# Rounded second-layer products, double-bank score tiles, moved copies, and five value loads by SyncE in a sparse attention with token routing

## The chip, the core and the metric

The program runs on one core of one Trainium2 chip. Its engines are named as the profile names them: PE (TensorE, matrix products; PEld is its loading of the stationary operand), DVE (VectorE), ACT (ScalarE), POOL (GpSimd) and SP (SyncE, which here only issues DMA transfers). A name with a q behind it (SPq, POOLq) is that engine's instruction queue. Each engine works through its own instructions in order, and engines wait for each other on semaphores. The metric is the device time of one execution in microseconds (us); smaller is better.

## What is computed

Four batches of block-sparse attention over 8 heads, 768 positions and 64 channels, and behind it a layer that routes the 128 highest-scored tokens of each batch through two dense layers. All inputs and outputs are f32.

```python
scores = scale * np.matmul(q, k.transpose(0, 1, 3, 2))
# blocks of 32; visible: |block_i - block_j| <= 1, first and last block (as row or column),
# and three sampled blocks for each block of queries (the same for all batches and heads)
scores = np.where(mask, scores, -1000000000.0)
attn = softmax(scores)                      # over the last axis
out = np.matmul(attn, v)                    # then x = out as [B, S, H * D]

scores = np.einsum('bsd,d->bs', x, w_gate)  # per token
top_idx = np.argpartition(-scores[b], 128)[:128]
xe = x[b, top_idx]
h = np.maximum(xe @ w1, 0.0)                # 512 -> 1024
ye = h @ w2                                 # 1024 -> 512
g = 1.0 / (1.0 + np.exp(-scores[b, top_idx]))
out[b, top_idx] = x[b, top_idx] + g[:, None] * ye
```

## The kernel before

**Steps.** A batch has 14 steps: three "g" steps for the first and last blocks of queries, which see all keys in three parts, and eleven units u = 1 to 11 of two query blocks each. All four batches make one list of 56 steps (`steps`, line 648). This text calls the batches one to four; the code counts b from 0. The loop from line 715 is a pipeline written out by hand: iteration s does, in this order on each engine,

- the loads and POOL work listed for s (`todo`, filled by `early`),
- `norm` of step s - 1 (DVE: divide by the sum; SP stores the rows), then the routing work listed under "a",
- `exps` of step s + 1, first half (ACT), then `turn(s)`: eight transposes of the probabilities on PE and their copies out of PSUM, the first by ACT, the second by ACT or, where `EVAC` says so (line 644), by DVE,
- `gate` of step s - 1 (DVE), routing work "c" of s - 1, `exps` of step s + 1, second half, routing work "aa", and ACT's work in `late`,
- `scores(s + 2)` and `out(s)` on PE, routing work "ab" and "b", `maxima` of step s + 2 (DVE), routing work "d".

Where nothing is late, PE is thus two steps ahead with the scores.

**PSUM.** `ps_s` holds the scores, four tiles of one bank, two to a step; `ps_t` the transposes; `ps_o` the attention output and small routing results; `ps_m` one bank for the two dense layers of batches one to three. In the last batch the dense layers use `ps_s`.

**Keys and values of a unit.** A unit's keys are gathered in SBUF into one of four buffers `kr` (line 236): two end blocks (`ends`, POOL), the four neighbouring blocks (`near`, a copy of 128 x 512, by ACT, or by POOL for u up to 4 in batches two to four), and six sampled blocks (`sampled`, POOL, at offsets that POOL loads into registers). Its values come in two parts: the fixed blocks `vs`, loaded by SP, and 2 x 128 rows `vr` (line 268), which POOL gathers from HBM with one indirect DMA for each of the unit's two query blocks (e = 0, 1) into one of seven buffers. POOL takes `gather` and `sampled` in turn, unit after unit (lines 677 to 680).

**Loads.** SP issues everything else, in program order: q two steps ahead of the scores that read it (line 685), the next batch's keys and fixed values from step 3 of the batch on (lines 686 to 690), the weights w1 and w2 (line 692), and both stores of every unit's rows. `load` ties the first transfer of a step to ACT's last instruction before it (`pace`).

**Routing.** `route(b)` places the routing of a batch into the loop by step and place (`at`, `run`): gate scores into rows and columns, ranks by comparison (`rank`, DVE), `sums`, `select`, `chosen`, `fetch` (an indirect DMA of the chosen rows by POOL). Then, from step `EXPERT[b]` on, `xt` (transpose), `h_mm` (first layer, f32), `relu` (ACT, line 582), `y_mm` (second layer, f32, line 587) and `put` (DVE, then an indirect store). The dense layers of batch one run in steps 28 to 38, of batch two in 39 to 49, of batch three in 50 to 60; those of batch four and what lies behind step 55 form the tail, in which the work is run in sorted order of step and place.

**Weights of the g steps.** `weights` (line 379) takes the running maximum over the three parts on DVE and its exponential `gw` on ACT, directly behind `next_maxima`; `join` of the next iteration begins with ACT's copy `gb`, which frees a transpose bank that PE's next transposes need.

## Time and profile before

| | us |
|---|---|
| median of three runs | 295.59 |
| the three runs | 293.88, 295.59, 297.04 |
| the profiled execution, its own time | 297.49 |
| its span, first to last instruction | 295.8 |
| mean granted PE clock | 0.991 |
| bytes read from HBM, written | 54.55 MB, 7.35 MB |

How to read the profile. The page gives for each engine the busy time, its share of the span and the number of instructions, and then the span in 40 equal slices, a digit for each slice in tenths of busy time. The chain is the work that ended last, followed back from the last instruction. In the order of time a line is start, duration, engine, line of the kernel (L66 is the helper that records every operation, so that groups are told apart by the names of their tiles), operation, output<-inputs, shape, count and, in brackets, how long the engine had been idle and what released it. In the groups the numbers behind the bar are busy time, mean nanoseconds of one and idle time before. A stretch is start:end, length, then for each engine busy time and number of instructions, the granted clock, the mean busy share of the 16 DMA engines and GB/s. An f32 product shows as two PE instructions.

### The profile page before, as it was taken

How to read it: one execution, taken by the hardware profiler on the slowest of the kernel's cores; microseconds unless marked ns; L12 is line 12 of the kernel's file. 1: busy time of each engine (PE TensorE's matmuls, PEld its weight loads, DVE VectorE, ACT ScalarE, POOL GpSimd, SP SyncE). 2: the span in 40 equal slices, each digit the busy share in tenths (PEclk: the TensorE clock that was granted, in tenths of full speed). 3: DMA queues.
4: the chain of work that ended last, by engine and by line, in shares of the span. 5: the costliest groups of instructions: out<-in, count | busy, mean ns of one | idle time of the engine just before them, and what ended most of it. 6: DMA issues, size and time to landing. Idle time of an engine off the chain costs nothing.

```text
span 295.8 us, 14282 instructions
## 1 busy us (share of the span) xinstructions
PE 259.0 (88%) x5824; PEld 192.3 (65%) x5824; DVE 204.5 (69%) x625; ACT 165.2 (56%) x392; POOL 198.2 (67%) x449
## 2 busy tenths in 40 slices
PE   3879997887988968988999999999999999889991
PEld 3456674665655745675777666787766578774890
DVE  3879886778799976884787666876995876653100
ACT  2477787563766675447467566566566576520100
POOL 5659999899998895999689616998689720011111
PEclk9799999999999999999999999999999999999998
DMA  5688899997778999989789985778466551011000
GB/s 186 232 288 265 248 361 333 331 282 213 196 211 276 288 336 367 272 275 289 239 267 296 322 254 165 241 221 219 137 177 184 141 180 39 21 39 35 38 17 19
DMA packets 33510, 62.84 MB, mean 212 GB/s; under 512 B 5284, under 2 KB 15780, under 8 KB 33444
## 3 DMA queue, kind: packets, MB, share of 16 engines
q1 hardware_dynamic: 25748, 36.39, 38.6%
q0 software_dynamic: 7696, 25.53, 28.0%
q8 instruction: 46, 0.75, 1.0%
q14 instruction: 20, 0.16, 0.2%
HBM read 54.55 MB, written 7.35 MB: 209 GB/s over the span
## 4 chain that ended last, share of the span: by engine, by line
PE 58%; DVE 20%; DMA 8%; ACT 6%; issue 5%; SPq 1%; POOLq 0%; POOL 0%; ACTq 0%; DVEq 0%
PE o L66 13%; PE h L66 10%; PE pt L66 10%; PE s L66 9%; PE y L66 8%; DVE mx L66 6%; DVE gm L66 4%; PE s_g L66 3%; DMA vr<-vt,vidx 2%; PE o_g L66 2%; DMA wbuf<-w 2%; DMA k<-kt 2%; PE pt_g L66 2%; DVE x L66 2%; ACT pr L66 1%
## 5 line engine op out<-in xcount | busy, mean ns | idle before, releaser
L66 POOL COPY kr<-k 128x128 f32 (+2 forms) x308 | 91.6, 336 | 19.1 <-DMA k<-kt 12.5
L66 POOL DMA_INDIRECT vr<-vt,vidx x88 | 89.0, 1011 | 19.4 <-issue 12.2
L66 ACT ACTIVATE pr<-s,mx 128x256 f32<-128x256 f32 x176 | 74.8, 483 | 37.0 <-DVE z L66 25.8
L66 DVE TENSOR_REDUCE mx<-s 128x2 f32<-128x512 f32 x88 | 56.5, 683 | 25.3 <-PE s L66 22.8
L66 ACT COPY pc<-pt 128x512 f32<-128x512 f32 x73 | 40.1, 592 | 17.9 <-PE pt L66 17.8
L66 PE MATMUL s<-kr,q 64*32 64x256 f32 x1408 | 48.8, 382 | 0.8 <-issue 0.8
L66 PE MATMUL pt<-ident,pr 128*128 128x128 f32 x352 | 47.2, 276 | 0.8 <-PE pt L66 0.8
L66 PEld LDWEIGHTS pt<-ident,pr 128*128 128x128 f32 x352 | 39.1, 141 | 7.2 <-issue 4.9
L66 PEld LDWEIGHTS o<-vs,pc 128*32 128x32 f32 (+1 forms) x1056 | 23.4, 118 | 27.1 <-ACT pc L66 17.8
L66 PE MATMUL o<-vs,pc 128*32 128x65 f32 (+1 forms) x1056 | 29.8, 224 | 8.8 <-ACT pc L66 3.3
L66 PE MATMUL h<-xT,wbuf 128*128 128x128 f32 x256 | 33.4, 281 | 1.3 <-ACT h L66 0.6
L66 PE MATMUL o<-vr,pc 128*32 128x65 f32 x1408 | 30.6, 222 | 3.9 <-DMA vr<-vt,vidx 2.1
L66 PEld LDWEIGHTS h<-xT,wbuf 128*128 128x128 f32 x256 | 30.1, 191 | 2.6 <-ACT h L66 0.8
L66 PE MATMUL y<-wbuf,h 128*128 128x512 f32 (+1 forms) x80 | 30.7, 521 | 0.7 <-ACT h L66 0.5
L66 PEld LDWEIGHTS s<-kr,q 64*32 64x32 f32 x1408 | 21.6, 106 | 14.2 <-issue 6.8
L66 ACT ACTIVATE pr_g<-s_g,gm 128x256 f32<-128x256 f32 x48 | 20.3, 485 | 13.8 <-DVE gm L66 9.2
L66 PEld LDWEIGHTS o<-vr,pc 128*32 128x32 f32 x1408 | 23.6, 109 | 6.1 <-DMA vr<-vt,vidx 2.4
L66 DVE CUSTOM_DVE_ANT_0 j<-x,wg_i 128x256 f32<-128x256 f32 x48 | 22.0, 459 | 0.8
L66 ACT COPY kr<-k 128x512 f32<-128x512 f32 x32 | 20.6, 643 | 0.0
L66 DVE TENSOR_TENSOR x<-o,z 128x256 f32<-128x256 f32 x44 | 18.7, 424 | 1.5
L66 PEld LDWEIGHTS y<-wbuf,h 128*128 128x128 f32 x80 | 14.1, 189 | 8.0 <-issue 5.8
L66 POOL CAST tb<-sc 128x6 bf16<-128x6 f32 x4 | 1.0, 243 | 27.3 <-DVE sc L66 27.3
(121 smaller groups left out, 309.8 us busy)
## 6 DMA issues: line engine op xcount, KB each, us to landing
vs<-vst SPq DMA_DIRECT2D x44, 260.0 KB
q<-qt SPq DMA_DIRECT2D x24, 256.0 KB
out<-x SPq DMA_DIRECT2D x88, 64.0 KB
wbuf<-w SPq DMA_DIRECT2D x16, 256.0 KB
k<-kt SPq DMA_DIRECT2D x21, 192.0 KB
vr<-vt,vidx POOLq DMA_INDIRECT x88, 4.7
k<-kt SPq DMA_DIRECT2D x3, 256.0 KB
k<-kt SPq DMA_DIRECT2D x1, 576.0 KB
```

What stands on the lines that cost most here:

```text
L66: i = getattr(self.engine, name)(*args, **kw)
```

## The change

It has these parts:

1. The score tiles become two tiles of two banks each, and one reduction takes all four maxima of a step.
2. The second dense layer is computed from rounded parts in the type float32r: w2 is split once into a rounded part (`w_high`, ACT) and the rest (`w_rest`, DVE), h in each batch likewise (`relu`: ACT the rounded part, DVE the rest), and `y_mm` multiplies high by high, high by rest and rest by high: 24 products for 8. The w2 rows are first loaded into staging tiles that share places with h; the rests lie in one key buffer and two value buffers, which the last units no longer use (`kr_at`, `vr_at`: three key buffers and five value buffers from there on). The weight loads stand at other steps.
3. `near` goes to POOL for all units of batch two and units 1 to 8 of batch three (batch four as before: 1 to 4); before, units 1 to 4 of each.
4. `EVAC` gives the second copy of every second step to DVE only in the first 14 steps (before: 28), later of every fourth.
5. The exponential of `weights` moves into `late` of the next iteration, behind both halves of `exps`.
6. `fetch` moves from place "c" to "a" of the same iteration in batches one to three, its sigmoid becomes `share` at "c", and the first subtraction of `select` becomes `ahead_of`; in the last batch the first `sums` stand one step earlier. `xt_out` and `relu` run at a new place "ar", behind `gate` and ahead of the second half of `exps`. One batch's times of `y_mm` differ.
7. In batch one the second gather (e = 1) of units 3, 5, 7, 9 and 11 becomes `plain`: SP loads three offsets into registers and issues four DMAs of 32 rows each, four steps ahead of the unit, ahead of that step's q, k and fixed value loads. DVE computes the offsets `voff` at the start.

```diff
-    ps_s = ctx.enter_context(tc.tile_pool(name="ps_s", bufs=4, space=PSUM))
+    ps_s = ctx.enter_context(tc.tile_pool(name="ps_s", bufs=2, space=PSUM))
...
+    voff = dup.bitcast(I32)[0:1]
+    vec.tensor_scalar(voff, rb[0:1], float(BLK), None, ALU.mult)
...
     def w_load(i):
         t, half = i % 4, i // 4 % 2
...
             f = i - 8
-            load(w2_s[:, f], w2[f * P:(f + 1) * P])
+            if f < 6 and f % 2 == 0:
+                t = rout.tile([P, 2, DM], F32, tag=f"h{min(f // 2, 1)}", name=f"w2_{f}")
+                stage[f], stage[f + 1] = t[:, 0], t[:, 1]
+            elif f >= 6:
+                stage[f] = rout.tile([P, DM], F32, tag="w2", name=f"w2_{f}")
+            load(stage[f], w2[f * P:(f + 1) * P])
+
+    def w_high(f):
+        act.copy(w2_h[:, f], stage[f])
+
+    def w_rest(f):
+        vec.tensor_tensor(w2_low(f), stage[f], w2_h[:, f], ALU.subtract)
...
+    KEND, VEND = 2 * NU - 4, 2 * NU - 2
+
+    def kr_at(n):
+        return n % KR if n < KEND else (n - KEND) % (KR - 1)
+
+    def vr_at(n):
+        return n % NV if n < VEND else (n - VEND + 1) % (NV - 2)
...
+    def w2_low(f):
+        tag, i = (("w2_0", 0) if f < 1 else (f"kr{KR - 1}", f - 1) if f < 4 else (f"vr{NV - 2 + (f - 4) // 2}", f % 2))
...
     def ahead(b, u):
-        return b and u <= 4
+        return u <= (0, NU - 1, 8, 4)[b]
...
+    def plain(u):
+
+        with tc.issue_after(sp.last):
+            _, o = nc.values_load_multi_w_load_instructions(
+                voff[0:1, 2 * u, :], engines=[SP], min_val=0, max_val=NB * BLK,
+                skip_runtime_bounds_check_because="sampled blocks index the blocks of the sequence")
+        j = NB if u == NU - 1 else 2 * u + 1
+        for i, rows in enumerate([slice(j * BLK, (j + 1) * BLK)] + [ds(x, BLK) for x in o]):
+            sp.dma_start(vr_of(0, u)[BLK * i:BLK * (i + 1), 1], vt[rows, :])
...
-        st[t] = [ps_s.tile([P, 2, 8, BLK], F32, tag="s", name=f"s{b}_{t[1]}_{t[-1]}_{g}") for g in range(G)]
+        st[t] = ps_s.tile([P, G, 2, 8, BLK], F32, tag="s", name=f"s{b}_{t[1]}_{t[-1]}")
...
-        for g in range(G):
-            vec.tensor_reduce(mx[:, g], st[t][g].rearrange("p h k c -> p h (k c)"), AX.X, ALU.max, negate=True)
+        vec.tensor_reduce(mx.rearrange("p g h -> p (g h)"), st[t].rearrange("p g h k c -> p (g h) (k c)"), AX.X, ALU.max,
+                          negate=True)
...
-        act.activation(d, d, AF.Exp)
+        late.setdefault(steps.index((b, "g", c)) - 1, []).insert(0, lambda: act.activation(d, d, AF.Exp))
...
-    Y_AT = ((7, 7, 8, 8, 9, 9, 10, 10),) * 2 + ((7, 8, 9, 9, 10, 10, 10, 10), (5, 5, 6, 6, 7, 7, 8, 8))
+    Y_AT = ((7, 7, 8, 8, 9, 9, 10, 10),) * 2 + ((7, 9, 9, 10, 10, 10, 10, 10), (5, 5, 6, 6, 7, 7, 8, 8))
...
+        def ahead_of():
+            R["rs"] = rout.tile([P, T], F32, tag="rs", name=f"rs{b}", bufs=2)
+            vec.tensor_tensor(R["rs"], later, R["cp"], ALU.subtract)
...
         def relu(k):
-            if k == 0:
-                R["h"] = rout.tile([P, 8, P], F32, tag="h", name=f"h{b}")
-            act.activation(R["h"][:, 4 * k:4 * k + 4], R["pm"], AF.Relu)
+            h = R["h", k] = rout.tile([P, 2, 4, P], F32R, tag=f"h{k}", name=f"h{b}_{k}")
+            act.activation(h[:, 0], R["pm"], AF.Relu)
+            vec.scalar_tensor_tensor(h[:, 1], R["pm"], 0.0, h[:, 0], ALU.max, ALU.subtract)
...
-            pe.matmul(R["y"][:, 0:c.stop - c.start], R["h"][:, f], w2_s[:, f, c], start=f == 0, stop=f == 7)
+            parts = [(0, f, w2_h[:, f, c]), (0, f, w2_low(f)[:, c])]
+
+            parts += [(1, i, w2_h[:, i, c]) for i in ((f,) if f < 4 else () if f < 7 else range(4, 8))]
+            for n, (i, j, w) in enumerate(parts):
+                pe.matmul(R["y"][:, 0:c.stop - c.start], R["h", j // 4][:, i, j % 4], w,
+                          start=f == 0 and n == 0, stop=f == 7 and n == len(parts) - 1)
...
-        plan += [(c, "c", lambda: rank(5)), (c if last else c + 1, "ab", lambda: sums(0, T - 1)),
-                 (c + 1, "ab", lambda: sums(T - 1, T)), (c + 1, "c", select), (c + 2, "ab", chosen), (c + 2, "c", fetch)]
+        plan += [(c, "c", lambda: rank(5)), (c - 1 if last else c + 1, "ab", lambda: sums(0, T - 1)),
+                 (c + 1, "ab", lambda: sums(T - 1, T)), (c + 1, "c", select), (c + 2, "ab", chosen)]
+        plan += [(c + 1, "bb", ahead_of), (c + 2, "c", fetch)] if last else [(c + 2, "a", ahead_of), (c + 3, "a", fetch), (c + 2, "c", share)]
...
-        return steps.index(t) % (2 if steps.index(t) < EXPERT[0] else 4) == 0
+        return steps.index(t) % (2 if steps.index(t) < per else 4) == 0
...
+    PLAIN = (3, 5, 7, 9, 11)
...
         for e in range(2):
-            early(at_, lambda b=b, u=u, e=e: gather(b, u, e))
+            if b == 0 and e and u in PLAIN:
+                early(max(at_, first[n] - 4), lambda u=u: plain(u))
+            else:
+                early(at_, lambda b=b, u=u, e=e: gather(b, u, e))
...
-    for i in range(16):
-        early((22 if i < 4 else 21 if i < 8 else 22) + i, lambda i=i: w_load(i))
+    for i, at_ in enumerate((20, 21, 22, 23, 27, 28, 29, 30, 24, 25, 26, 28, 33, 33, 31, 34)):
+        early(at_, lambda i=i: w_load(i))
+    for f, at_ in enumerate((31, 31, 32, 32, 34, 34, 33, 36)):
+        late.setdefault(at_, []).append(lambda f=f: w_high(f))
+        at(at_, "d", lambda f=f: w_rest(f))
...
+        run(s, "ar")
         run(s - 1, "c")
```

More of the change, by code (lines that the diff above doesn't have):

```diff
@@ L8 @@
 F32 = mybir.dt.float32
+F32R = mybir.dt.float32r
 BF16 = mybir.dt.bfloat16
@@ L16 @@
 POOL = mybir.EngineType.Pool
+SP = mybir.EngineType.SP
 ACT = mybir.EngineType.Activation
@@ L216, in load_gate @@
             sp.dma_start(wg_i[64 * g:64 * g + 64], wg2[:, g * 256:(g + 1) * 256].broadcast_to([64, 256]))
-    wbuf = const.tile([P, 2 * DM * FF // P], F32, name="wbuf")
-    w1_s = wbuf[:, 0:DM * FF // P].rearrange("p (t f) -> p t f", f=FF)
-    w2_s = wbuf[:, DM * FF // P:].rearrange("p (f c) -> p f c", c=DM)
+    w1_s = const.tile([P, DM // P, FF], F32, name="w1_s")
+    w2_h = const.tile([P, FF // P, DM], F32R, name="w2_h")
+    stage = {}
     def w_load(i):
@@ L228, in w_load, with user_of, vr_of @@
             f = i - 8
-            load(w2_s[:, f], w2[f * P:(f + 1) * P])
-    offs = {}
-    kbuf = [const.tile([P, 14, KW], F32, name=f"kr{i}") for i in range(KR)]
-    def kr_of(b, u):
-        return kbuf[(b * (NU - 1) + u - 1) % KR]
+            if f < 6 and f % 2 == 0:
[8 more added lines that the diff above has]
+        vec.tensor_tensor(w2_low(f), stage[f], w2_h[:, f], ALU.subtract)
+    offs = {}
+    kbuf = [const.tile([P, 14, KW], F32, tag=f"kr{i}", name=f"kr{i}") for i in range(KR)]
+    KEND, VEND = 2 * NU - 4, 2 * NU - 2
[3 more added lines that the diff above has]
+        return n % NV if n < VEND else (n - VEND + 1) % (NV - 2)
+    def user_of(place, n):
+        return max((i for i in range(n) if place(i) == place(n)), default=None)
+    def kr_of(b, u):
+        return kbuf[kr_at(b * (NU - 1) + u - 1)]
+    vbuf = [const.tile([P, 2, VR], F32, tag=f"vr{i}", name=f"vr{i}") for i in range(NV)]
+    def vr_of(b, u):
+        return vbuf[vr_at(b * (NU - 1) + u - 1)]
+    lows = {}
+    def w2_low(f):
+        tag, i = (("w2_0", 0) if f < 1 else (f"kr{KR - 1}", f - 1) if f < 4 else (f"vr{NV - 2 + (f - 4) // 2}", f % 2))
+        if tag not in lows:
+            n = DM if f < 1 else 14 * KW if f < 4 else 2 * VR
+            lows[tag] = const.tile([P, n], F32R, tag=tag, name=f"low_{tag}")
+        return lows[tag][:, DM * i:DM * (i + 1)]
     def offsets(b, u):
@@ L253, in ahead @@
     def ahead(b, u):
-        return b and u <= 4
+        return u <= (0, NU - 1, 8, 4)[b]
     def ends(b, u):
-        if u <= KR:
+        if u <= (KR if b < 2 else KR - 1):
             for at in (4, 8):
@@ L302, in scores @@
                         qe = q[rows, p].rearrange("d e c -> d (e c)") if ne == 1 else q[rows, p, e]
-                        pe.matmul(st[t][g][r0:r0 + w, ph], qe, keys(rows, e, slice(p * BLK, (p + 1) * BLK)),
+                        pe.matmul(st[t][r0:r0 + w, g, ph], qe, keys(rows, e, slice(p * BLK, (p + 1) * BLK)),
                                   start=ph == 0, stop=ph == 1, tile_position=(64 * g, r0), skip_group_check=True)
@@ L362, in out @@
             return
-        parts = [(1 if b < 2 else 2, lambda e: vs_of(b, t[1])), (2, lambda e: vrs[b, t[1]][:, e])]
+        parts = [(1 if b < 2 else 2, lambda e: vs_of(b, t[1])), (2, lambda e: vr_of(*t)[:, e])]
         for c, (ne, v) in enumerate(parts):
@@ L552, in fetch, with share @@
                     vec.tensor_scalar(R["put"][:, half:half + 1], ts[:, 0:1], 2.0, float(half), ALU.mult, ALU.add)
+            R["ts"] = ts
+            if last:
+                share()
+        def share():
             ge = R["ge"] = rout.tile([P, 1], F32, tag="ge", name=f"ge{b}", bufs=2)
-            act.activation(ge, ts[:, 1:2], AF.Exp, scale=-1.0)
+            act.activation(ge, R["ts"][:, 1:2], AF.Exp, scale=-1.0)
             vec.tensor_scalar_add(ge, ge, 1.0)
@@ L558, in mid @@
         def mid(name):
-            pool = (ps_s, "s") if b == B - 1 else (ps_m, "m")
-            return pool[0].tile([P, 512], F32, tag=pool[1], name=f"{name}{b}").rearrange("p (t c) -> p t c", t=4)
+            if last:
+                m = ps_s.tile([P, 1024], F32, tag="s", name=f"{name}{b}")[:, 0:512]
+            else:
+                m = ps_m.tile([P, 512], F32, tag="m", name=f"{name}{b}")
+            return m.rearrange("p (t c) -> p t c", t=4)
         def xt():
@@ L671, in block_sparse_attention_moe @@
         m = n + 2 if b == 0 else n
-        at_ = max(first[m - KR] - 1 if m >= KR else 0, first[n - NV] + 1 if n >= NV else 0, b2 * per - 3)
+        k_, v_ = user_of(kr_at, m), user_of(vr_at, n)
+        at_ = max(0 if k_ is None else first[k_] - 1, 0 if v_ is None else first[v_] + 1, b2 * per - 3)
         if b:
@@ L677, in block_sparse_attention_moe @@
         for e in range(2):
-            early(at_, lambda b=b, u=u, e=e: gather(b, u, e))
+            if b == 0 and e and u in PLAIN:
+                early(max(at_, first[n] - 4), lambda u=u: plain(u))
+            else:
+                early(at_, lambda b=b, u=u, e=e: gather(b, u, e))
             if u2 < NU:
```

14 lines of the change are left out of this document (5 added, 9 removed).

## The prediction

> **What bounds the kernel now.** I read the page first (shares, slices, chain), then the stretches of the four batches, then the order of time where TensorE idles, then the groups by shape for prices. Work runs in 56 steps, 14 to a batch (3 global, 11 units); a stretch below starts at the first transpose of its batch.
>
> ```profile
> span 295.8 us, 14282 instructions
> PE   3879997887988968988999999999999999889991
> POOL 5659999899998895999689616998689720011111
> PE 58%; DVE 20%; DMA 8%; ACT 6%; issue 5%; SPq 1%; POOLq 0%; POOL 0%; ACTq 0%; DVEq 0%
> ```
>
> ```profile
> core 0: us, PE busy (x) PEld busy (x) DVE busy (x) ACT busy (x) POOL busy (x), PEclk, DMA share, GB/s
> 12.10:67.50 55.40, 48.42 (x1238) 34.86 (x1239) 43.89 (x131) 40.29 (x96) 47.03 (x102) 1.00 0.89 290
> 67.50:126.90 59.40, 49.76 (x1275) 35.76 (x1273) 50.12 (x149) 37.36 (x91) 51.75 (x117) 1.00 0.87 272
> 126.90:196.90 70.00, 66.14 (x1567) 49.62 (x1566) 50.44 (x158) 42.59 (x101) 52.48 (x116) 1.00 0.81 254
> 196.90:258.40 61.50, 59.30 (x1449) 44.89 (x1448) 44.90 (x141) 38.87 (x92) 34.71 (x75) 1.00 0.50 146
> 258.40:295.80 37.40, 29.11 (x247) 22.52 (x245) 8.78 (x30) 3.98 (x9) 5.36 (x8) 0.98 0.09 29
> ```
>
> Batches three and four are TensorE's: busy 66.14 of 70.00 us and 59.30 of 61.50. There only fewer matmul microseconds help. In batch one TensorE idles 7.0 us (55.40 - 48.42), in batch two 9.6 us; in two VectorE (50.12) and POOL (51.75) are as busy as TensorE, so those waits come from them. The last stretch is a serial tail: route the last tokens, fetch, two matmul layers, store.
>
> **The change part by part.**
>
> *Five gathers leave POOL (units 3, 5, 7, 9, 11 of batch one).* Around the sixth to eighth unit POOL never rests, and TensorE waits for a gather that POOL issued late:
>
> ```profile
> 42.64 0.98 POOL L66 DMA_INDIRECT vr<-vt,vidx  x1 [0.16 <-issue]
> 43.61 0.76 POOL L66 COPY kr<-k 128x128 f32 x3
> 44.54 0.98 POOL L66 DMA_INDIRECT vr<-vt,vidx  x1 [0.16 <-issue]
> ```
>
> ```profile
> 44.54 6.73 DMA vr<-vt,vidx
> ```
>
> ```profile
> PE o L66 <- DMA vr<-vt,vidx: 2.1, 2, 1.7
> PE pt_g L66 <- ACT gb L66: 3.0, 3, 1.2
> ```
>
> A gather takes POOL 0.98 + 0.16 = 1.14 us, so five free 5.7 us of the 47.03. Only two waits, 2.1 us in all, are ended by a gather; at most the whole 7.0 us idle could go, at least nothing. I take 2.1: two of the removed gathers precede the first wait, three the second, so POOL is 2.3 to 3.4 us earlier there, more than the waits.
>
> What they become is put on SyncE: per unit a register load and four copies of 32 rows, 25 instructions, placed ahead of that step's q, k and value loads and its output stores.
>
> ```profile
> 39.92 0.53 SPq L66 DMA_DIRECT2D k<-kt  x1
> 40.49 0.48 SPq L66 DMA_DIRECT2D vs<-vst  x1
> 41.07 1.12 SPq L66 DMA_DIRECT2D out<-x  x2
> 43.15 0.33 SPq L66 DMA_DIRECT2D q<-qt  x1
> 9.37 0.18 DVE L66 TENSOR_SCALAR koff<-rb 1x72 int32<-1x72 f32 x1
> L243 POOLq TENSOR_LOAD <-koff x44: 1384/1395/2465, 9.6 to 233.0; - x44
> ```
>
> No SyncE register load is in the trace; the nearest row is POOL's, 1.4 us. It costs nothing if it runs behind other issues, 2.5 us at worst. Four issues at 0.45 us (between the 0.33 of q and the 0.56 of an output store) are 1.8 us; together 3.2 us every second step. SyncE issues 0.53 + 0.48 + 1.12 = 2.1 us a step, 2.3 with its half share of a q load; two steps at TensorE's 3.3 us hold 6.6, and the demand becomes 4.6 + 3.2 = 7.8. So SyncE falls 1.2 us behind in every pair of steps, 4 to 5 us by the tenth step. Behind it wait q (issued two steps, 6.6 us, ahead of its scores, of which a landing as slow as the 6.73 above leaves nothing, one of 4 some 2 us) and batch two's k and fixed value loads. I charge +1.0 us, from 0 (backlog hidden) to +3. The offsets themselves cost VectorE one more multiply like koff's, 0.18 us at the start; between 0 and that, I book 0.
>
> The Trainium skill, DMA: Bandwidth & Descriptors, section "Issuing engines are not separate DMA queues", speaks against this part: the same 16 engines move the bytes whoever issues, so only issue time is saved. By that rule alone the 2.1 us would be 0, and the sum 2.1 us less; the trace is open on it, for issue time is what POOL lacked, while the bytes are the same.
>
> *Weights' exponentials later (gw).* ScalarE now waits for VectorE's weight before it copies gb, and TensorE's next transposes wait for that copy: 3.0 us in three waits (row above). With gw behind the next exps, gb starts when its matmuls are done. I take 2.0 of the 3.0, 0.7 in each of batches one to three (rounded in the sum); 0 if another wait ends last.
>
> *One maximum reduction over two banks, fewer VectorE evacuations, near copies to POOL, two score tiles of double size instead of four.*
>
> ```profile
> L66 DVE TENSOR_REDUCE mx<-s 128x2 f32<-128x512 f32 x88 | 56.5, 683 | 25.3 <-PE s L66 22.8 <-ACT pr L66 2.1
> L66 DVE COPY pc<-pt 128x512 f32<-128x512 f32 x15 | 10.3, 685 | 5.6 <-PE pt L66 5.5
> L66 POOL COPY kr<-k 128x512 f32<-128x512 f32 x12 | 7.4, 617 | 0.0
> L66 ACT COPY kr<-k 128x512 f32<-128x512 f32 x32 | 20.6, 643 | 0.0
> 98.65 1.01 POOL L66 COPY kr<-k 128x128 f32 x3
> 102.34 0.88 PE L66 MATMUL s<-kr,q 64*32 64x256 f32 x24
> ```
>
> A pair of reductions occupies 56.5/44 = 1.28 us; one of 1024 columns is 683 + 512 more columns (0.53 at the pair's slope, 0.6 busy each), 1.21, so 0.07 saved a step: 1.0 in batch two. Batch two loses four evacuations (steps 14, 18, 22, 26 go to ScalarE): 4 x 0.685 = 2.7. Of this 3.7 us of VectorE's 50.12 I let half shorten the batch, 1.9. ScalarE takes four copies and gives up seven near copies of 643 ns. Both tiles of a step were already waited for together, so the tiles cost nothing.
> POOL gets those seven near copies: 7 x 0.617 = 4.3 us, in a batch where it is 87% busy. For the eighth unit its copies end at 99.66, TensorE reads them at 102.34: margin 2.7 us. POOL enters batch two some 3 us earlier (5.7 freed, less a wait for the k loads that SyncE's backlog makes late), and by unit eight has spent 4 x 0.617 = 2.5 of it. So the margin is 3.2 us, and that caps what both batches gain together: of -2.1 + 1.0 - 0.7 - 1.9 - 0.7 = -4.4 I book **-3.2**. In batches three and four POOL has room (its ring shrinks to three key and five value buffers; at 52.48 of 70.00 and 34.71 of 61.50 busy I cost that at nothing; uncovered, each late unit would cost its 1 us gather).
>
> *The second layer in rounded parts.* Eight f32 products of 512 columns become 24 (high x high, high x low, low x high).
>
> ```profile
> L66 PE MATMUL y<-wbuf,h 128*128 128x512 f32 x48 | 23.7, 616 | 0.7 <-ACT h L66 0.5 <-issue 0.2
> L66 PE MATMUL y<-wbuf,h 128*128 128x256 f32 x32 | 7.1, 379 | 0.0
> 166.60 1.82 PE y L66 x4
> 172.04 1.91 PE y L66 x4
> L66 DVE SCALAR_TENSOR_TENSOR xe<-y,ge,xe 128x512 f32<-128x512 f32 x3 | 2.3, 751 | 2.7 <-PE y L66 2.7
> L66 DVE TENSOR_TENSOR ga<-ga,gb 128x260 f32<-128x260 f32 x8 | 3.6, 456 | 0.8
> 144.40:163.20 18.80, 18.42 (x480) 14.77 (x479) 15.08 (x49) 12.04 (x27) 16.05 (x36) 1.00 0.85 268
> ```
>
> An f32 product is two instructions (48 for 24 products) of 0.455 to 0.478 us: 16 x 0.466 = 7.46 us a batch. The new type is in no row. Bounds: 0.455 an instruction (as now) or half, 0.228 (if one instruction that no longer splits the moving operand streams at twice the pace). I take 0.228: the pair shows an f32 operand being split, and the other operand should be split alike. Then 24 x 0.228 = 5.47, -2.0 a batch, **-4.0** for the experts of batches one and two, which run in the TensorE-bound stretches. It breaks even at 7.46/24 = 0.311 us.
> The Trainium skill, FP8 and Floating Point Precision, section "TensorE Precision Notes", counts four passes for true FP32; a quarter of the 0.93 us product is 0.23, the lower bound again; no run here shows it.
> Added: eight ScalarE roundings of w2 (643 ns each, 5.1 us, steps 31 to 36) and eight VectorE subtractions: 456 ns at 260 columns plus 252 more columns is 0.72, 5.8 us. Also two VectorE low parts per batch at 0.75. In 144.4 to 163.2 (steps 31 to 34) VectorE is free 3.7 us of 18.8; seven subtractions and a low part bring 5.8: it overruns by about 2. I charge **+2.0** (0 if steps overlap, 4 if the order chains them). ScalarE (12.04) has 6.8 us free and gives up four near copies in this batch. SyncE's loads for f = 4, 5, 7 wait for the subtractions of the step before; out stores queue behind; x has six buffers: nothing.
> Relu and xT copies moved ahead of the second exps end TensorE waits of about 0.5 us; gw gives 0.6: batches three and four together -4.0 + 2.0 - 0.6 - 0.5 = **-3.1**.
>
> *The tail.*
>
> ```profile
> 266.22 0.52 PE L66 MATMUL scp<-one_b,M 128*128 128x1 bf16 x15
> 266.60 1.10 PE L66 MATMUL y<-wbuf,h 128*128 128x512 f32 x2
> 267.54 0.29 PE L66 MATMUL scp<-one_b,M 128*128 128x1 bf16 x6
> 267.87 0.16 DVE L66 TENSOR_TENSOR rs<-later,scp 128x6 f32<-128x6 f32 x1 [1.86 <-PE scp L66]
> 274.88 7.42 PE L66 MATMUL h<-xT,wbuf 128*128 128x128 f32 x64 [0.46 <-ACT xT L66]
> ```
>
> The first sums move one place up and batch three's y products leave the gap before the last sums: rs, 1.86 us late, comes 1.0 earlier, and the fetch with it. The first layer (7.42) stays. The last y, 7.1 us for 32 instructions, becomes 48 of 256 columns; half of 0.222 is 0.111, but 64 loads and products of 128 columns take 7.42/64 = 0.116, which I take as the floor: 5.57, -1.5. The low parts finish under the products. Tail **-2.5**.
>
> Sum: -3.2 - 3.1 - 2.5 = **-8.8 us**. The profiled execution took 297.49 us (span 295.78 and 1.7 around it), so 288.7; it stands 1.9 above the median of the three runs, 295.59. Against the median: **286.8 us**.
>
> **The rivals.**
> 1. *Neither POOL nor VectorE limits.* SyncE hides the loads, POOL stays ahead, the w2 work overlaps: -2.8 in batch one, -4.4 in two, -5.1 in three and four, -2.5: -14.8, **280.8 us**. For it: the copies' margin is still 2.7 us where POOL is deepest in batch two. Against: margin has to carry 4.3 us of new copies.
> 2. *The moved rows are late all the same*, on SyncE's queue or on the DMA engines (0.89 busy in batch one, the bytes unchanged). Then batches one and two give nothing: -5.6, **290.0 us**; with q late too, 292. For it: 7.8 us of issue in 6.6.
> 3. *The other side: the new products stream no faster than an f32 instruction.* One mechanism: 24 x 0.455 = 10.9 a batch, +3.5 instead of -2.0, for two batches +11 against my sum; in the tail 48 x 0.217 = 10.4, +3.3 instead of -1.5, and the gap before the sums fills again, +1.5. Total +8.5: **304.1 us**. It decides above 0.311 us an instruction. For it: no f32 row here passes a column in under 0.89 ns (0.455 us for 512). Against: only that the operands are rounded to one part, which the trace does not show.
>
> **How the numbers follow.** Forecast 0.47, rival one 0.18, rival two 0.20, rival three 0.08, something else 0.07. Range 280 to 294 us: it takes in rivals one and two and leaves out rival three and half of the rest. About 1% (3 us) is what a measurement of this kernel can tell from no change: faster is below 292.6. That is nearly all of the forecast, all of rival one and most of two: 0.77; within 1%, the ends of two and some of the rest, 0.12; slower, rival three and the rest, 0.11.
>
> **What would show each step.** y instructions near 0.23 us and 72 plus 48 of them; no TensorE wait for vr at the seventh unit; SyncE's issues in steps 3 to 9 and whether scores wait for q; POOL's last key copies of batch two against the scores; VectorE overrunning in steps 31 to 36; rs one microsecond sooner after the last rank. Wrong would be: y at 0.45, scores waiting for q or kr for more than 3 us, or batch one not shorter.

## The result and the profile after

| | before | after |
|---|---|---|
| median, us | 294.00 (293.62 to 297.04, 6 runs) | 299.69 (297.42 to 301.52, 6 runs) |
| ratio, 95% interval | | 1.0147 (1.0104 to 1.019) |
| the profiled execution, us | 297.49 | 299.08 |
| its mean granted clock | 0.991 | 0.97 |

The change made the kernel slower by 1.5%. The prediction, 286.8 us with a range to 294, was wrong in size and in sign. The medians lie 5.7 us apart, the two profiled executions only 1.6: the one of before was 3.5 us above its median, the one after 0.6 below. The traces below therefore show where 1.6 us went; the other 4.1 are in no trace. On two chips of the experiments the same kernel was faster than before; that comes further down.

The page of the changed kernel: shares, two engines and the clock in slices, and its chain, which breaks off at the last store and so says nothing here.

```profile
span 297.4 us, 14386 instructions
PE   3899897949888899998997989999999999998891
POOL 6649998229999999999789685991888783003111
PEclk9999997987999999999997999999999999999996
issue 1%; POOLq 0%; DMA 0%
```

The stretches of the four batches and the tail, cut at the first transposes of each as before.

```profile
core 0: us, PE busy (x) PEld busy (x) DVE busy (x) ACT busy (x) POOL busy (x), PEclk, DMA share, GB/s
12.03:73.94 61.91, 53.19 (x1239) 38.35 (x1239) 43.55 (x117) 39.91 (x96) 42.55 (x100) 0.92 0.84 260
73.94:130.54 56.60, 50.53 (x1275) 36.30 (x1273) 48.90 (x132) 35.82 (x88) 52.72 (x113) 1.00 0.88 282
130.54:201.28 70.74, 66.73 (x1575) 53.24 (x1574) 56.17 (x153) 44.52 (x104) 58.71 (x125) 0.98 0.81 257
201.28:261.90 60.62, 58.26 (x1456) 46.63 (x1455) 44.06 (x127) 38.58 (x93) 34.49 (x75) 1.00 0.50 143
261.90:297.40 35.50, 26.94 (x271) 23.77 (x269) 11.61 (x37) 3.97 (x9) 5.34 (x8) 0.94 0.10 30
```

Batch one is 6.5 us longer (61.91 against 55.40), batch two 2.8 shorter, batch three 0.7 longer, batch four 0.9 shorter, the tail 1.9 shorter. Together +1.6, the difference of the two profiled executions. POOL's busy time in batch one fell from 47.03 to 42.55 as intended, and two of its slices show a 2: it waits there. The clock of batch one is 0.92 where it was 1.00.

In the order of time, TensorE's two long waits of batch one, then SyncE's queue around them, then POOL:

```profile
46.72 1.63 PE L68 MATMUL s<-kr,q 64*32 64x256 f32 x32 [2.65 <-DMA q<-qt]
66.19 1.99 PE L68 MATMUL s_g<-k,q 64*64 64x256 f32 x16 [4.13 <-DMA q<-qt]
```

```profile
38.95 3.30 SPq L68 DMA_DIRECT2D vr<-vt  x4
42.37 1.18 SPq L68 DMA_DIRECT2D q<-qt  x1
...
48.28 3.37 SPq L68 DMA_DIRECT2D vr<-vt  x4
51.75 0.37 SPq L68 DMA_DIRECT2D q<-qt  x1
...
58.12 3.95 SPq L68 DMA_DIRECT2D vr<-vt  x4
62.17 0.37 SPq L68 DMA_DIRECT2D k<-kt  x1
62.59 0.42 SPq L68 DMA_DIRECT2D vs<-vst  x1
63.06 0.42 SPq L68 DMA_DIRECT2D q<-qt  x1
```

```profile
64.78 1.29 POOL L68 COPY kr<-k 128x256 f32<-128x256 f32 x3 [10.89 <-DMA k<-kt]
```

Scores wait for q, 2.65 us in step 8 (7.40 us long, 4.02 before) and 4.13 us in step 12 (9.24 us, 3.26 before). The q loads that should go out as steps 6, 8 and 10 begin (35.86, 42.98 and 53.80 us here) go out at 42.37, 51.75 and 63.06: 6.5, 8.8 and 9.3 us behind. In the kernel before, the q load of step 8 goes out at 43.15, 0.5 us after the step begins. A row `vr<-vt x4` holds a unit's register load and its four issues. From one such row to the next, 38.95 to 48.28, SyncE works without a pause for 9.3 us, while the two steps 6 and 7 take 7.1. The next batch's last keys go out at 62.17, and POOL, which had gained its head start, loses it in one wait of 10.89 us.

Each wait is paid twice: within 2 us of its end the granted clock halves, for one or two stretches of 3.41 us. Three stretches, cut where the clock changes:

```profile
47.16:50.57 3.41, 3.41 (x75) 2.31 (x58) 1.47 (x3) 0.40 (x2) 3.08 (x11) 0.50 1.02 371
64.22:71.05 6.83, 4.86 (x68) 3.45 (x69) 2.55 (x5) 0.76 (x2) 5.70 (x14) 0.50 0.89 253
159.80:163.21 3.41, 3.41 (x16) 3.41 (x17) 3.27 (x9) 0.84 (x2) 3.24 (x7) 0.50 1.04 373
```

That is 13.65 us at half clock. In batch one TensorE is busy for 8.3 us of it, work that takes about half of that at full clock: some 4 us, an estimate from these rows. The third stretch is step 33 (8.72 us, 5.14 before). There VectorE and ScalarE show why:

```profile
152.77 0.68 DVE L68 SCALAR_TENSOR_TENSOR h<-h,h 128x512 fp32r<-128x512 f32 x1
153.37 0.70 DVE L68 SCALAR_TENSOR_TENSOR M<-sb,sc,before 128x384 bf16<-128x384 f32 x1
...
154.00 0.74 DVE L68 SCALAR_TENSOR_TENSOR M<-sb,sc,before 128x512 bf16<-128x512 f32 x1
...
154.67 1.21 DVE L68 TENSOR_REDUCE mx<-s 128x4 f32<-128x1024 f32 x1
...
156.12 1.28 DVE L68 TENSOR_TENSOR low_kr<-w,w_h 128x512 fp32r<-128x512 f32 x2
```

```profile
156.30 0.84 ACT L68 ACTIVATE pr<-s,mx 128x256 f32<-128x256 f32 x2 [2.38 <-DVE mx L68]
```

The low part of h and two comparisons stand ahead of the reduction whose maxima ScalarE waits for, 2.38 us, and two rests of w2 follow it; products of step 33 stand behind ScalarE.

The groups that answer to the prices of the prediction (busy, mean ns of one, idle before):

```profile
L68 DVE TENSOR_REDUCE mx<-s 128x4 f32<-128x1024 f32 x44 | 53.6, 1219 | 23.7 <-PE s L68 22.4 <-issue 1.2
L68 DVE SCALAR_TENSOR_TENSOR h<-h,h 128x512 fp32r<-128x512 f32 x8 | 5.5, 690 | 14.0 <-ACT h L68 12.8 <-ACT pc L68 1.2
```

The merged reduction takes 1.22 us (1.21 forecast). The low parts of h take 0.69 each, and VectorE waits 12.8 us for ScalarE ahead of them. Of the waits for ScalarE's gb, 3.0 us before, TensorE has none of its own left.

### The profile page after: what moved, and what is told of

Same layout as the page of the kernel before. It is cut to its first block, busy times and chain, and to the rows that moved or that the text cites. A ratio compares the mean times of both kernels' runs of the same rounds, so it can differ in the third digit from the quotient of the medians.

```text
span 297.4 us, 14386 instructions
## 1 busy us (share of the span) xinstructions
PE 262.3 (88%) x5864; PEld 203.0 (68%) x5864; DVE 210.4 (71%) x582; ACT 164.9 (55%) x393; POOL 200.6 (67%) x451
## 2 busy tenths in 40 slices
DMA packets 34069, 62.83 MB, mean 211 GB/s; under 512 B 5524, under 2 KB 16020, under 8 KB 34004
## 5 line engine op out<-in xcount | busy, mean ns | idle before, releaser
L68 POOL COPY kr<-k 128x128 f32 (+2 forms) x315 | 97.9, 348 | 29.4 <-DMA k<-kt 12.6
L68 POOL DMA_INDIRECT vr<-vt,vidx x83 | 83.5, 1006 | 21.0 <-issue 12.0
L68 DVE TENSOR_REDUCE mx<-s 128x4 f32<-128x1024 f32 x44 | 53.6, 1219 | 23.7 <-PE s L68 22.4
L68 PE MATMUL s<-kr,q 64*32 64x256 f32 x1408 | 50.6, 385 | 4.0 <-DMA q<-qt 2.8
L68 PE MATMUL h<-xT,w_s 128*128 128x128 f32 x256 | 34.7, 289 | 0.9 <-ACT xT L68 0.5
L68 PEld LDWEIGHTS h<-xT,w_s 128*128 128x128 f32 x256 | 31.6, 200 | 2.1 <-ACT xT L68 0.7
L68 PE MATMUL y<-w_h,h 128*128 128x512 f32 (+1 forms) x80 | 23.5, 364 | 0.8 <-DVE sc L68 0.8
L68 PE MATMUL s_g<-k,q 64*64 64x256 f32 x192 | 16.4, 472 | 7.9 <-DMA q<-qt 4.1
L68 DVE TENSOR_REDUCE gm<-s_g 128x4 f32<-128x1024 f32 x12 | 14.7, 1222 | 11.5 <-PE s_g L68 11.5
L68 PEld LDWEIGHTS o_g<-vs,pc_g 64*64 64x64 f32 x384 | 13.8, 136 | 7.8 <-ACT pc_g L68 5.1
```

The source lines that it names most:

```text
L68: i = getattr(self.engine, name)(*args, **kw)
```

## The experiments

Eighteen measurements were made on five chips, called A to E; some kernels ran on several. On A, B, C and E the kernel before took 314 to 319 us, on D 295. So ratios are always to the kernel before on the same chip, and absolute times are compared within one chip only.

| kernel | chip | before, us | this, us | ratio, 95% interval |
|---|---|---|---|---|
| without the five loads | A | 318.46 | 312.48 | 0.9851 (0.9749 to 0.9952) |
| before, with the five loads alone | A | 318.46 | 317.97 | 0.9986 (0.9942 to 1.0031) |
| loads behind q, k and values | A | 318.46 | 308.31 | 0.970 (0.9589 to 0.981) |
| loads of fixed rows | A | 318.46 | 308.65 | 0.9717 (0.9635 to 0.9799) |
| the whole change | B | 318.87 | 309.51 | 0.9808 (0.9691 to 0.9925) |
| without the five loads | B | 318.87 | 310.83 | 0.9824 (0.9695 to 0.9953) |
| before, with the five loads alone | B | 318.87 | 318.02 | 0.9989 (0.9925 to 1.0052) |
| loads behind q, k and values | B | 318.87 | 309.25 | 0.9732 (0.9602 to 0.9861) |
| the whole change | C | 314.00 | 309.29 | 0.985 (0.9802 to 0.9898) |
| loads behind, ranks sooner | C | 314.00 | 310.16 | no interval given |
| the same, relu on VectorE | C | 314.00 | 309.09 | 0.9849 (0.9768 to 0.993) |
| the kernel before, once more | C | 314.00 | 315.36 | one run |
| nine loads instead of five | D | 295.06 | 310.97 | 1.0537 (1.0481 to 1.0593) |
| less work in batch one, five loads | D | 295.06 | 296.36 | 1.0032 (0.9988 to 1.0076) |
| less work in batch one, no loads | D | 295.06 | 291.23 | 0.9867 (0.9802 to 0.9932) |
| the second layer in f32 | D | 295.06 | 299.36 | 1.0151 (1.0079 to 1.0222) |
| without the five loads | E | 314.40 | 309.83 | 0.9861 (0.9806 to 0.9916) |
| the same, ranks sooner, relu on VectorE | E | 314.40 | 307.03 | 0.9768 (0.9716 to 0.9821) |

**Without the loads, and the loads alone (chip A).** The first takes the seventh part out of the change:

```diff
-    PLAIN = (3, 5, 7, 9, 11)
+    PLAIN = ()
```

> The whole change but for its seventh part: all second gathers of batch one stay on POOL. Theory A (the loads that SyncE now issues delay q and the next keys, and the granted clock falls behind the waits): batch one is back near 55 us, no half clock before step 33, no score product waits for q; 291 to 294 us, against 299.7 for the whole change and 294 before. Rival B (the other six parts make it slow): 297 or more, with the same waits of PE in another place of batch one.

The second puts `plain`, `voff` and the branch in the list of gathers into the kernel before, and nothing else.

> The kernel before with the seventh part alone. Theory A: PE waits for q in steps 8 to 12, two windows of half clock, batch one 4 to 7 us longer than its 55.4; 298 to 301 us. Rival B: within 1 us of before, 293 to 295.

Neither answer of theory A came: on this chip the loads alone cost nothing (317.97 against 318.46), and the change without them is 1.5% faster than before. Rival B does not hold either: it asked for a version without the loads slower than before. And before takes 318 us here, 24 more than in the result, so this is another condition.

**Order and amount of SyncE's work (chip A).** The loads are registered behind those of their step, or read fixed rows without the register load:

```diff
-                early(max(at_, first[n] - 4), lambda u=u: plain(u))
+                behind.append((max(at_, first[n] - 4), u))
...
+    for s, u in behind:
+        early(s, lambda u=u: plain(u))
```

> The whole change, with each unit's register load and four issues placed behind that step's q, k and value loads in SyncE's order instead of ahead of them. If the order in the queue is what hurts, q is issued some 3 us sooner in the steps that have both, and half or more of the loss comes back: 294 to 296 us, with the keys of batch two still late. If it is the total time of issue, or the bytes on the DMA engines, that hurts: 298 to 300.

```diff
-        with tc.issue_after(sp.last):
-            _, o = nc.values_load_multi_w_load_instructions(
...
-        for i, rows in enumerate([slice(j * BLK, (j + 1) * BLK)] + [ds(x, BLK) for x in o]):
+        for i, rows in enumerate([slice(j * BLK, (j + 1) * BLK)] + [slice(x * BLK, (x + 1) * BLK) for x in (2 * u - 1, 2 * u, 2 * u - 3)]):
```

> The whole change, with the four loads of 32 rows at fixed addresses and no register load; it reads other rows, so the values of these blocks are not the sampled ones, but the bytes are the same. SyncE saves the load of 0.7 to 0.9 us and the register arithmetic, about 1.2 of some 3.3 us for each of the five. If the issue time counts, the demand of 7.8 us in 6.6 falls to 6.6: 294 to 296 us. If the bytes on the DMA engines count, or the wait for the buffer: 298 to 300.

308.3 and 308.7 us, but the whole change had no time on this chip, so these two decide nothing by themselves.

**The whole beside its parts (chip B).** No new edit.

> The whole change, unaltered, beside its parts on one chip. The chip of the first four kernels ran the kernel before in 318.5 us, with 11 to 14 us of TensorE waits that nothing in the profile ends, so only kernels of one chip are compared. Theory A (the loads ahead of the queue cost 5 to 7 us, the rest gains): slower than before by 1 to 2%, and slower than the same change without these loads by 1.5 to 3%. Rival B (the other six parts make it slow): the same time as without these loads, within 1%.

> The whole change without its seventh part, again, beside the whole change. Theory A: 1.5 to 3% under the whole change, 0.5 to 1.5% under the kernel before. Rival B: level with the whole change. Rival D (the loads help once they are behind the queue, as 308.3 against 312.5 us on the first chip hints): above the version with the loads behind by 1%.

> The kernel before with the seventh part alone, again. On the first chip it was level with the kernel before (ratio 0.9986, 0.9942 to 1.0031), which speaks against theory A, if waits of another kind did not hide the loss there. Theory A: 1 to 2.5% slower than before here. Rival B: level again.

> The whole change with the loads behind the q, k and value loads of their step, again, beside the whole change. If the order in SyncE's queue is the cause: 1 to 2% under the whole change and under the kernel before. If the amount of issue or the bytes are: level with the whole change.

The whole change is 1.9% faster than before here, level with the version without the loads (309.5 and 310.8) and with the loads behind (309.3). Theory A, as first stated, has fallen: the same loads cost nothing on this chip. What differs is above all TensorE's pace. Rows of SyncE's queue in the whole change on chip B:

```profile
42.04 0.36 SPq L68 DMA_DIRECT2D q<-qt  x1
47.87 3.28 SPq L68 DMA_DIRECT2D vr<-vt  x4
51.43 0.19 SPq L68 DMA_DIRECT2D q<-qt  x1
56.47 3.55 SPq L68 DMA_DIRECT2D vr<-vt  x4
61.24 0.42 SPq L68 DMA_DIRECT2D q<-qt  x1
```

These q loads go out at 42.0, 51.4 and 61.2 us, hardly sooner than in the result (42.4, 51.8, 63.1). But steps 6, 8 and 10 begin at 38.36, 46.10 and 55.94 instead of 35.86, 42.98 and 53.80, so the loads are 3.7, 5.3 and 5.3 us behind and the scores hardly reach them: the only wait for q in batch one is 1.1 us. In the kernel before with the loads alone the q loads of these steps are 4 to 7 us late on chips A and B, and scores wait 1.5 and 2.6 us for them.

**Why chips A, B, C and E are slower.** The kernel before was profiled on chip C, beside the whole change and two repairs.

> The whole change once more, beside the kernel before and two changed versions on one chip. On the second chip it was 2% faster than before (309.5 against 318.9 us), on the chip of the result 1.5% slower. Theory A' (the loads ahead of the queue cost time only where TensorE is fed without gaps: there the steps last 3.3 us and SyncE's demand of 7.8 us does not fit into two of them; where gaps stretch the steps to 3.8 us and more, it fits): if before runs near 294 us here, this one is slower than it by 1 to 2% with stalls for q in steps 8 and 12; if before runs near 318, it is 1 to 3% faster and those stalls are under 2 us. Rival C (the stalls come from chance, not from the pace): slow in some executions of both chips alike, so its own times here spread by 5 us or more.

> The kernel before, for its trace on this chip. If it runs near 294 us, TensorE's waits that nothing ends are 5 us as in the profile shown; if near 318, some 12 us, spread over batches one to three, and the steps of batch one last 3.8 us or more in the mean.

Step 49 of the kernel before, on TensorE: first in the profile shown ahead of the prediction, then on chip C.

```profile
233.51 0.67 PE L66 MATMUL o<-vs,pc 128*32 128x65 f32 x32
234.00 0.64 PE L66 MATMUL o<-vr,pc 128*32 128x65 f32 x32
```

```profile
249.12 0.73 PE L66 MATMUL o<-vs,pc 128*32 128x65 f32 x16
250.27 0.33 PE L66 MATMUL o<-vs,pc 128*32 128x65 f32 x4 [0.42 <-issue]
251.00 0.44 PE L66 MATMUL o<-vs,pc 128*32 128x65 f32 x12 [0.40 <-issue]
251.23 0.67 PE L66 MATMUL o<-vr,pc 128*32 128x65 f32 x32
```

The same 64 products take 1.1 us in the one and 2.8 us in the other, with gaps in which TensorE waits for nothing that is recorded. In the list of waits of before on chip C and in the profile shown, in this order, this kind of wait is:

```profile
PE o L66 <- issue: 9.8, 24, 1.1
```

```profile
PE o L66 <- issue: 1.8, 1, 1.8
```

Over all tiles such waits are 5.4 us in the profile shown, 2.1 in the result, 1.3 to 4.6 on chip D, and 11 to 15 on A, B, C and E. What makes them is open: the packets of the largest DMA queue take 0.071 us in the mean on A and B as in both profiles of the result, which speaks against slower transfers, and no experiment was made on it. Batch one of the kernel before lasts 64.3 us on chip C and 55.4 in the profile shown. Of these 8.9 us such gaps make up 3.7 (4.2 against 0.5), and the granted clock is 0.95 instead of 1.00; the rest is not explained.

The other two kernels of chip C test step 33, both with the loads behind as well:

```diff
-            plan += [(c, "c", lambda: rank(0)), (c + 1, "c", lambda: rank(1)), (c + 2, "c", lambda: rank(2)),
+            one = int(b == 1)
+            plan += [(c, "c", lambda: rank(0)), (c + 1 - one, "c", lambda: rank(1)), (c + 2 - one, "c", lambda: rank(2)),
...
```

> The whole change with the loads behind q, k and values in their step, and with the comparisons `rank(1)` and `rank(2)` of batch two one step sooner, so that VectorE has one comparison of 0.70 us less in the step ahead of step 33. If VectorE's queue is what makes step 33 long (8.7 us in the result, 7.0 on the second chip, 5.1 before), it falls by 0.7 us or, where half clock goes too, by 3: 0.3 to 1% under the whole change, and 2% or more under it on a chip on which the loads hurt. If something else makes it long, it stays at 7 or more.

```diff
-            act.activation(h[:, 0], R["pm"], AF.Relu)
+            if b:
+                vec.tensor_scalar(h[:, 0], R["pm"], 0.0, None, ALU.max)
+            else:
+                act.activation(h[:, 0], R["pm"], AF.Relu)
```

> As the kernel with the sooner ranks, and in batches two to four VectorE computes the rounded part of h too, so that its low part does not wait for ScalarE (12.8 us of such waits, the longest ahead of the last stretch 2.5 us). If that wait delays the maxima, steps 43, 44, 46 and 47 are shorter by 1 us together or more; if VectorE's added 0.68 us each takes that back, the time is level.

Step 33 goes from 7.05 us to 6.66 and 6.62, so VectorE's queue sets part of it, but by less than the 0.7 us expected, and the times stay level (310.2 and 309.1 against 309.3). With the relu on VectorE steps 43, 44, 46 and 47 change by -0.1, -0.6, +0.1 and +0.3 us, 0.3 shorter together, not the 1 us expected if the wait for ScalarE delayed the maxima there. The whole change itself is 1.5% faster than before on this chip, with one wait for q of 2.3 us. Its times spread by 7.6 us, which rival C would ask for, but those of before spread by 6.8, so the spread tells nothing.

**The dose and the pace (chip D).** This chip runs the kernel before in 295.06 us, as in the result. The first kernel uses the loads for all of the units 3 to 11; the next two leave products out of batch one so that it runs faster:

```diff
-    PLAIN = (3, 5, 7, 9, 11)
+    PLAIN = tuple(range(3, NU))
```

> The whole change with the loads by SyncE for all nine units 3 to 11 of batch one instead of every second. SyncE's demand is then 2.3 + 3.2 = 5.5 us a step. Theory A' (SyncE's issue time against TensorE's pace): it fits into no pace, the backlog grows by 1.5 us in each of nine steps even at 4 us a step, and TensorE waits for q or the next keys for 8 us or more in all: 6 to 14 us above the whole change. Rival C (the stalls were chance): within 2 us of the whole change, with POOL 4 us freer.

```diff
-        for c, (ne, v) in enumerate(parts):
+        for c, (ne, v) in list(enumerate(parts))[int(b == 0):]:
...
```

> The whole change, with the value products of the fixed rows left out in the units of batch one (half of each unit's value products), so that TensorE has less to do there and reaches the pace of 3.3 us a step or less that it had in the result. Theory A': stalls for q appear near steps 8 and 12 as in the result, of 4 us or more in sum, and batch one is no shorter than the 58.7 us of the whole change on the third chip, or by less than 3. Rival C: no such stalls, batch one some 5 us shorter.

The third is the same with `PLAIN = ()`.

> The same products left out, without the loads by SyncE. Theory A': no wait for q; batch one shorter than that of the kernel with the loads by 3 us or more, if POOL's second gathers (some 50 us of work) do not become the bound; if they do, TensorE waits for gathered rows or key copies instead, and the two are level within 2 us. Rival C: level with no stall in either.

Nine loads take 310.97 us, 15.9 above before, where five took 5.7. The dose acts, and it acts where theory A' says: stretches of batch one with nine loads, and the waits for q and key copies in it.

```profile
12.02:82.97 70.95, 54.12 (x1239) 38.23 (x1239) 43.01 (x117) 40.22 (x96) 38.40 (x97) 0.86 0.77 228
```

```profile
PE s_g L68 <- DMA q<-qt: 5.1, 1, 5.1
PE s L68 <- DMA q<-qt: 5.0, 1, 5.0
PE s L68 <- POOL kr L68: 3.4, 1, 3.4
```

POOL is freer than ever (38.40 us) and the DMA engines idler (0.77 of their time, 228 GB/s), yet the stretch is the longest of all. So neither POOL nor bytes bound it; SyncE's queue does, in which the q loads of steps 6, 8 and 10 go out 11 to 15 us late.

The pair with less work shows the price of the five loads on one chip: 296.36 with them, 291.23 without, 5.1 us between the medians. The two profiled executions differ by only 0.8 us (291.86, the fastest of its ten, and 291.11), so their stretches show where time moves, not the whole price. Batch one and batch two with the loads, then without:

```profile
12.13:69.72 57.59, 46.34 (x1062) 31.77 (x1063) 43.61 (x117) 39.56 (x96) 42.30 (x99) 0.94 0.87 272
69.72:125.67 55.95, 50.49 (x1278) 36.02 (x1274) 48.34 (x132) 35.58 (x88) 52.04 (x113) 1.00 0.90 295
```

```profile
13.01:65.34 52.33, 43.21 (x1062) 29.75 (x1062) 42.75 (x117) 39.76 (x96) 44.22 (x95) 0.97 0.90 298
65.34:124.23 58.89, 50.91 (x1276) 36.18 (x1274) 49.50 (x132) 35.58 (x88) 54.65 (x119) 1.00 0.88 282
```

Batch one is 5.3 us longer with the loads, batch two 2.9 us shorter. Two points of what was expected were not met. The 58.7 us named there is not batch one of the whole change on chip C, which took 62.8, so the comparison with that chip says little; the one with the next kernel does. And only 0.9 us of TensorE's wait is put down to q with the loads. Waits for transposed tiles are alike in both (4.7 and 4.2 us), and a wait of 1.9 us for a key copy of ScalarE is there only with the loads; so this pair shows a price, but not by itself that q is what carries it. The q loads are again 5.3 to 8.9 us behind their steps with the loads (40.56, 49.16 and 59.35 for steps that begin at 35.27, 42.16 and 50.49) and at most 1.4 without. Without them waits for gathered rows appear, 2.6 us, as theory A' had allowed.

**The second layer (chip D).** The whole change with w2 and h left as f32 and eight products:

```diff
-            parts = [(0, f, w2_h[:, f, c]), (0, f, w2_low(f)[:, c])]
-
-            parts += [(1, i, w2_h[:, i, c]) for i in ((f,) if f < 4 else () if f < 7 else range(4, 8))]
+            parts = [(0, f, w2_h[:, f, c])]
...
```

> The whole change with the second layer in f32 as before (eight products, no rounding of w2 or h on ScalarE and VectorE). By the prediction's terms: 2.0 us more in each of batches two and three's stretches and 1.5 in the tail, 2.0 less in steps 31 to 36: 3.5 us above the whole change. By what the result showed (0.64 us gained in steps 46 to 49, step 33 longer by 3.6): steps 31 to 36 2 us or more shorter, steps 46 to 49 under 1 us longer, the tail 1.5 to 2 longer: level with the whole change within 1.5 us.

Its ratio, 1.0151, is level with that of the whole change in the result, 1.0147, within 0.8%: no gain of the rounded layer is seen at this pace. Batch one, which has no product of that layer, is here a second trace of the five loads beside their queue: it lasts 59.7 us, the q loads of steps 6, 8 and 10 go out 6.7, 8.4 and 8.9 us late, and TensorE waits for them three times:

```profile
PE s L68 <- DMA q<-qt: 5.5, 3, 2.4
```

The tail is 0.7 us longer than in the result (36.21), not 1.5. By stretches, steps 31 to 36 and steps 39 to 49 of this kernel:

```profile
147.04:174.88 27.84, 27.82 (x702) 20.92 (x701) 22.97 (x66) 16.44 (x38) 24.25 (x53) 1.00 0.84 270
184.71:237.56 52.85, 51.80 (x1223) 38.70 (x1221) 39.53 (x112) 32.26 (x78) 40.56 (x88) 1.00 0.60 176
```

Steps 31 to 36 with the rounded layer (the kernel with nine loads, same chip, clock 1.00), and steps 39 to 49 of the result:

```profile
159.06:189.32 30.26, 27.52 (x706) 21.77 (x705) 28.39 (x76) 20.36 (x46) 26.93 (x55) 1.00 0.81 257
```

```profile
187.26:240.10 52.84, 51.53 (x1230) 40.66 (x1229) 39.78 (x114) 32.00 (x77) 40.23 (x86) 1.00 0.60 175
```

In steps 31 to 36 VectorE goes from 22.97 of 27.84 us to 28.39 of 30.26: it becomes the busiest engine, and the steps are 2.4 us longer. In steps 39 to 49 the two are equal to 0.01 us, although the products are cheaper: TensorE's time in them falls by 1.3 us in steps 46 to 49 (7.73 to 6.44), and its busy time over all eleven steps by only 0.3.

**The two repairs together (chip E).** Without the loads, and the same with the sooner ranks and the relu on VectorE.

> The whole change without the loads by SyncE. If before runs near 295 us here: theory A' gives batch one 55 to 57 us instead of 61.9, no wait for q, 293 to 295 us, ratio 0.99 to 1.00, where the whole change has 1.0147; rival B gives 1.01 or more. If before runs near 315: 0.98 to 0.985 as on the first two chips, which adds nothing.

> As m1, with two comparisons of batch two one step sooner and the rounded part of h on VectorE in batches two to four. If VectorE's queue took the gain back: step 33 shorter by 0.7 us or, where half clock goes too, by 3; steps 46 and 47 shorter by 0.5 us together; 1 to 4 us under m1, the fastest of all where before runs near 295. If it is something else: level with m1 within 1 us.

Before takes 314.4 us here, so the first adds nothing on the pace, as said. 307.03 against 309.83 us; the intervals (0.9716 to 0.9821 and 0.9806 to 0.9916) just overlap. Steps 33, 44, 46 and 47 are shorter by 0.35, 1.4, 1.0 and 0.5 us, step 48 is longer by 0.6: less than expected in step 33, more in 46 and 47. On chip C the same relu made steps 46 and 47 0.4 us longer together, so this gain is not shown to be its doing. The tail is 1.4 us longer (37.38 against 35.97). From the start of the last batch's first layer (283.41 and 290.06 us) both need 20.0 us to the end, so the difference lies ahead of it, where this kernel has 3.41 us at half clock (from 275.15) and the other none. Of the versions without the loads it is the fastest by ratio; with the loads behind their queue, A and B gave 0.970 and 0.973. None of these was run where before takes 295 us, so none is shown to beat both kernels there.

## Why the prediction was wrong

**The five loads.** The step that failed is "So SyncE falls 1.2 us behind in every pair of steps, 4 to 5 us by the tenth step [...] I charge +1.0 us, from 0 (backlog hidden) to +3". The mechanism was named, q and the next keys behind a full queue, and even the margin was there, some 2 us. The size was wrong. The price of a unit's loads was right (3.3 to 4.0 us for a register load and four issues, 3.2 forecast), but the rest of SyncE's work in two steps came to 6.0 us instead of 4.6, so SyncE falls 2.2 us behind in a pair of steps (9.3 of work in 7.1, steps 6 and 7), not 1.2, and the queue is 5.0 us behind already at the fourth step, 6.5 at the sixth and 9.3 at the tenth. The two waits for q are 6.8 us where +1.0 was charged. The prediction's terms for batch one add up to -1.8 us (-2.1, +1.0, -0.7); measured is +6.5, a miss of 8.3 and the largest of all. Batch two was to give -2.6 and gave -2.8. For the whole kernel the pair on chip D puts the five loads at 5.1 us by its medians. Rival two saw the right place and stopped at "batches one and two give nothing".

The Trainium skill, DMA: Bandwidth & Descriptors, section "Issuing engines are not separate DMA queues", says that another issuing engine saves issue time alone, and that this time is usually small beside the transfer. The trace agrees with the first and not with the second: the bytes are the same (62.84 and 62.83 MB), and the register load and four issues, 3.3 to 4.0 us a unit, fill a queue on which batch one waits.

**The clock.** No term stood for it. Two waits for q of 2.65 and 4.13 us put 10.2 us of batch one at half clock, some 4 us by the estimate above.

**The second layer's products.** Their rate was right: 0.23 us for 512 columns, and the last y fell from 7.1 us to 6.0 (5.6 forecast). The step that failed is "-4.0 for the experts of batches one and two, which run in the TensorE-bound stretches". Steps 35 to 38 and 46 to 49 gained 0.3 to 0.9 us instead of 2.0 each. Part of it is size: TensorE's time in these products fell by 1.3 us a batch, not 2.0. In steps 31 to 36 VectorE becomes the busiest engine with the low parts and the rests of w2. What holds back steps 46 to 49 is open: the low parts wait for ScalarE there, but taking that wait away made steps 46 and 47 together 1.5 us shorter on chip E and 0.4 longer on chip C. The charge for the rests, +2.0, was right (2.4 on chip D), and half clock in step 33 came on top in the result.

Rival three rested on a reading that does not hold: the last y of the kernel before passes 256 columns in 0.22 us, 0.86 ns each, so a row under 0.89 ns was there.

**Right in number.** Batch two is 2.8 us shorter, and POOL's copies were in time (TensorE waits 0.7 us for them). That the merged maxima, fewer evacuations and gw did this is not shown: no experiment takes one of them out, and in the pair on chip D, where both kernels have them, batch two takes 55.95 us with the five loads and 58.89 without. Some of the 2.8 us may thus be batch one's loss given back, which would be luck. The tail gained 1.9 of 2.5: rs came 0.5 us sooner, not 1.0.

**The sum by stretches.** Batches one and two +3.7 (forecast -3.2), three and four -0.1 (-3.1), tail -1.9 (-2.5): +1.6 against -8.8 on the profiled executions, +5.7 on the medians.

**On the other chips.** There the whole change is 1.5 to 1.9% faster than before. The loads alone cost nothing there; that gaps and half clock stretch TensorE's steps until SyncE nearly keeps up fits the traces, but no experiment made the gaps come or go. On chip C steps 46 to 49 of the kernel before take 24.0 us with f32 products and 21.5 in the whole change, of which 0.7 are fewer gaps; no kernel on these chips differs in the second layer alone, so what it gives there is not shown. The forecast's sign is right on these chips by luck: it was worked out for the faster pace and knew nothing of the gaps. Taking the 5.1 us of chip D from the 299.69 of the result gives 294.6, level with before: an estimate, since the change without the loads did not run on a chip of that pace.

## What to carry to other kernels

Count a queue's issue time per period against the period of the engine that it feeds, at the fastest pace the kernel reaches, and compare the backlog with how far ahead the loads are issued; once it exceeds that, charge all of it and the halved clock behind the wait. Before moving matmul work into cheaper products, see whether the engine that prepares the operands has room in the same steps. Where one kernel takes 295 us on one chip and 318 on another, compare edits on one chip, and look at the pace before believing a sign.

## What the hardware showed besides

A register load on SyncE takes 0.7 to 0.9 us, not the 1.4 of POOL's; the issues and their waits make up the rest of a unit's 3.5 us.

The clock halved after stretches in which TensorE had been idle for only part of the time. In the 3.41 us ahead of the half clock at 47.16, 64.22 and 159.80 it was busy 0.76, 1.24 and 1.63 us. In the whole change on chip B half clock at 54.78 came even after 2.15 busy us of 3.41, while on chip C, counting on in steps of 3.41 us from the half clock at 22.01, the stretch from 66.38 has 1.56 busy us and full clock follows. So no threshold comes out of these traces. The Trainium skill, TensorE: Matmul & The Clock Gate, section "Part 1: The HAM clock gate (the "warmup" mystery)", gives a free-running window of about 3.4 us, with which the stretches of 3.41 and 6.83 us agree, and half clock after an idle window; here windows with 0.76 to 2.15 us of work were followed by it too.

A product of 512 columns of float32r starts every 0.23 us, half of an f32 instruction and a quarter of an f32 product of two. The gaps in TensorE's work, 11 to 15 us on four of five chips and most of them among the value products, were not expected and are not explained.
